# Moving four phi units out of the retention loop into the routing chain, and the first expert's w1 loads and splits ahead of the branch

## The chip, the cores and the metric

The kernel runs on one core of a Trainium2 chip. The metric is the device time of one launch in microseconds (us). TensorE (PE) multiplies matrices, PEld loads its weights, VectorE (DVE), ScalarE (ACT) and GpSimd (POOL) work element by element, SyncE (SP) issues most DMA transfers. Each engine works through its own instructions in order.

## The reference

Three stages are chained; everything is float32.

- Retention over 4 batches, 8 heads, 768 positions: `state = gamma * state + k v^T`, `y = q state / 8`. Its output is `x` with 3072 tokens of 512 features.
- A mixture of 8 experts with one expert per token: `e = argmax(x w_gate)`, then `relu(x w1[e]) w2[e]` times the gate probability and a sigmoid of `x w_output_gate`.
- A soft mixture: `logits = x phi` (32 slots), a softmax over tokens gathers slot inputs, 8 experts of 4 slots each transform them, a softmax over slots combines them.

## The kernel before

**Retention loop.** 24 iterations, one per tile of 128 tokens. SP loads 1 MB per tile (`load`), PE computes scores (L408), the output (L432, L441) and the state (L455). After every third tile the gates follow: `gate_mm` (L491), an ACT copy, `gate_sum` (L506), a chain of small DVE operations up to `sb` (L557), and `scale_mm` (L573), which needs `sb`. The tiles are written to DRAM as `xs` (`x_put`, L623).

**Phi units.** The soft mixture's logits need `w2[e] phi`, which doesn't depend on tokens. It is cut into 32 units of 512 KB of w2, four per expert (`wq_mm`, L232); after the fourth unit `wq_turn` transposes the sum on DVE and `wq_put` (L240) stores it. Units 0 to 15 run in the loop (`wq_load` in iteration i, `wq_mm` in iteration i+2), 16 to 23 are loaded in pairs of 1 MB in the loop's last four iterations and multiplied at its end, 24 to 31 run in the expert loop (`wq_early`, `wq_late`).

**Routing chain.** After the loop DVE counts and ranks the tokens, sorts the experts by size (`ordi`), and makes the row numbers `xidx`; POOL gathers the first expert's tokens from `xs` (`gather(0)`, L716). DVE then makes `limi`, the number of tokens over an expert's capacity.

**The branch.** Every engine loads `limi` into a register (L735), compares it with 0 and jumps over the overflow code (L825; the jump is taken with these inputs).

**Expert loop.** For each expert and each of 8 slices of 128 hidden units (a step g): `load_w` brings 256 KB of w1 (L209, three buffers `r1`), `split_w` makes a high part on ACT (L218) and a low part on DVE (L219), `l1` multiplies the three products on PE (L880, 12 matmuls) and ACT applies the relu (L885). Before the first step `x_mm` transposes the gathered tokens on PE (L858) and `x_split` splits them.

The order on each engine is written out by hand, as the calls stand. Each DMA of SP and ACT is given one of eight lanes in turn (DMAHW0 to 7), and is issued only when the earlier DMA of the same lane has landed.

Of the kernel before, what the change touches and what calls it, by code (L numbers as in the profile page):

```python
# [9 lines left out]
F32 = mybir.dt.float32  # L10
F32R = mybir.dt.float32r
BF16 = mybir.dt.bfloat16
I32 = mybir.dt.int32
ACTF = mybir.ActivationFunctionType
ALU = mybir.AluOpType
AX = mybir.AxisListType
# [5 lines left out]
DM = H * D  # L22
E = 8
FF = 1024
NS = 32
NCH = S // 128
NTILE = NT // 128
KD = DM // 128
# [7 lines left out]
NPRE, NX = 48, 4  # L36
NH = 8
NQ = 4 * E
NQL, NQ0 = 16, 24
GROUPS = [(t, 3) for t in range(0, 21, 3)] + [(21, 2), (23, 1)]  # L40
ENDS = {t + n - 1: (t, n) for t, n in GROUPS}
ORDER = "xe sc s m g1 gc xr w rr rs g2 G0 Gb q oq os st G1 rc rk xw k".split()
# [94 lines left out]
def retention_moe_kernel(ctx, tc, qt, kt, kn, vn, gates, moe_w1, moe_w2,  # L137
# [33 lines left out]
    pos = per.tile([128, NTILE], I32, name="pos")  # L171
    rt = per.tile([128, 3, E], F32, name="rt")
    ordi = per.tile([1, E], I32, name="ordi")
    cnt, ordf, over = (rt[:, i, :] for i in range(3))
    mrun = per.tile([128, 1], F32, name="mrun")
    srun = per.tile([128, 1], F32, name="srun")
# [15 lines left out]
    def load_er(k):  # L192
        if k < E:
            er.append(nc.values_load(ordi[0:1, k:k + 1], engines=[mybir.EngineType.SP], min_val=0, max_val=E - 1))
# [30 lines left out]
    def wq_mm(u, pool, tag):  # L225
        if not 0 <= u < NQ:
            return
        e, kk = divmod(u, 4)
        if kk == 0:
            wacc[e] = pool.tile([128, 256], F32, tag=tag, name="wps")  # L230
        for g, t in enumerate(wtt.pop(u)):
            nc.tensor.matmul(out=wacc[e][32 * g:32 * g + 32, :], lhsT=phi[:, kk, :], rhs=t,  # L232
                             start=(kk == 0), stop=(kk == KD - 1), skip_group_check=True)
# [33 lines left out]


    with ExitStack() as pa:
        io = pa.enter_context(tc.tile_pool(name="io", bufs=5))  # L270
        sc2 = pa.enter_context(tc.tile_pool(name="sc2", bufs=2))
        one = pa.enter_context(tc.tile_pool(name="one", bufs=1))
        pT = pa.enter_context(tc.tile_pool(name="pT", bufs=1, space=PSUM))

# [44 lines left out]
                                         scale=dc[:, c - 2, q:q + 1])  # L319

        wst = pa.enter_context(tc.tile_pool(name="wst", bufs=4))

        def wq_load(i):

            if i % 5 < 4 and i // 5 * 4 + i % 5 < NQL:
                e, q = divmod(i // 5 * 4 + i % 5, 4)
                t = wst.tile([128, FF], F32, tag="wt", name="wt")
                nc.sync.dma_start(out=t, in_=moe_w2[1, e, :, q * FF:(q + 1) * FF])
                wtt[4 * e + q] = [t[:, g * 256:g * 256 + 256] for g in range(4)]
            elif NTILE - 4 <= i < NTILE:  # L330
                e, q = divmod(NQL + 2 * (i + 4 - NTILE), 4)
                t = io.tile([128, 4 * DM], F32, tag="raw", name="wt2")
                nc.sync.dma_start(out=t, in_=moe_w2[1, e, :, q * FF:(q + 2) * FF])
                for h in range(2):
                    wtt[4 * e + q + h] = [t[:, h * FF + g * 256:h * FF + g * 256 + 256] for g in range(4)]

        def wq_at(i):
            if 2 <= i < 22 and (i - 2) % 5 < 4:
                return [(i - 2) // 5 * 4 + (i - 2) % 5]
            if NTILE - 2 <= i:  # L340
                return [NQL + 2 * (i + 2 - NTILE), NQL + 2 * (i + 2 - NTILE) + 1]
            return []
# [3 lines left out]
                wq_mm(u, pT, "w")  # L346
                wq_turn(u)

        def wq_early(u):

            if NQ0 <= u < NQ:
                e, q = divmod(u, 4)
                wtt[u] = []
                for h in range(2):
                    t = m2a.tile([128, 512], F32, tag="m2", name="wte")
                    nc.sync.dma_start(out=t, in_=moe_w2[1, e, :, q * FF + h * 512:q * FF + h * 512 + 512])
                    wtt[u] += [t[:, 0:256], t[:, 256:512]]

        def wq_turn(u):
            if u % 4 == 3 and 0 <= u < NQ0:  # L360
                pool, tag = (wraw, "r1") if u == NQ0 - 1 else (sc2, "ws")
                wput[u // 4] = pool.tile([128, KF, NS], F32, tag=tag, name="ws")
                nc.vector.transpose(out=wput[u // 4], in_=wacc.pop(u // 4).rearrange("p (f t) -> p f t", t=32))

        raw, k2, q2, sps, sS, Ops, xT3, xr3, gps, gts, gs, scl, gr, oz = ({} for _ in range(14))
# [168 lines left out]
        def gate_own(i):  # L534
            if i not in ENDS:
                return
            t, n = ENDS[i]
            sm = gs[t]
            og = gps[t][:, LG:LG + 16 * n].rearrange("p (u e) -> p u e", e=16)[:, :, E:2 * E]
            one_ = lambda k: sm[:, k, 0, 0:n]  # L540
            big = lambda k: sm[:, k, 0:n, :]
            nc.vector.tensor_tensor(out=big(4), in0=og, in1=oh[:, t:t + n, :], op=ALU.mult)
            nc.vector.tensor_reduce(out=one_(5), in_=big(4), axis=AX.X, op=ALU.add)
            nc.scalar.activation(out=one_(7), in_=one_(5), func=ACTF.Exp, scale=-1.0)
# [38 lines left out]
        def rank(i):  # L583
            if i not in ENDS:
                return
            t, n = ENDS[i]
            eng = nc.vector if t + n == NTILE else nc.gpsimd
            g = gps.pop(t)
            sm = sc2.tile([128, 3, 4, E], F32, tag="sm2", name="sm2")
            nc.vector.tensor_tensor(out=sm[:, 0:n, 0, :], in0=g[:, RK:RK + E * n].rearrange("p (u e) -> p u e", e=E),  # L590
                                    in1=oh[:, t:t + n, :], op=ALU.mult)
            ps = pos[:, t:t + n]
            with nc.allow_low_precision(reason="a single whole number under 2 ** 24 among zeros"):
                nc.vector.tensor_reduce(out=ps, in_=sm[:, 0:n, 0, :], axis=AX.X, op=ALU.add)
            lo = sc2.tile([128, 3], I32, tag="lo", name="lo")[:, 0:n]
            hi = sm[:, 0, 2, 0:n]
            nc.vector.tensor_scalar(out=lo, in0=ps, scalar1=127, scalar2=None, op0=ALU.bitwise_and)
            nc.vector.tensor_tensor(out=hi, in0=ps, in1=lo, op=ALU.subtract)
            nc.vector.tensor_tensor(out=lcol[:, t:t + n, 1, :], in0=each(con("code"), n), in1=bc(hi, n, 32), op=ALU.is_equal)
            eng.tensor_tensor(out=lcol[:, t:t + n, 0, :], in0=lcol[:, t:t + n, 1, :], in1=bc(con("till")[:, t:t + n], n, 32), op=ALU.mult)  # L600
            eng.tensor_scalar(out=lcol[:, t:t + n, 1, :], in0=lcol[:, t:t + n, 1, :], scalar1=con("row"), scalar2=None, op0=ALU.mult)
            nc.vector.tensor_tensor(out=lrow[:, t:t + n, :], in0=each(con("i128"), n), in1=bc(lo, n, 128), op=ALU.is_equal)
# [14 lines left out]
        def x_put(i, queues=(nc.sync,)):  # L617
            if i not in ENDS:
                return
            t, n = ENDS[i]  # L620
            x = xr3.pop(t)
            for a in range(4):
                queues[a % len(queues)].dma_start(  # L623
                    out=xs[t * 128:(t + n) * 128, a * 128:(a + 1) * 128].rearrange("(b q) d -> q b d", q=32),
                    in_=x[32 * a:32 * a + 32, 0:n].rearrange("q u b d -> q (u b) d"))
# [35 lines left out]
        i = NTILE - 1  # L661
        wq_put(0)
        x_put(i - 1, (nc.sync, nc.scalar))
        gate_own(i)
        for u in wq_at(NTILE):
            wq_mm(u, pT, "st")
# [1 line left out]
        nc.tensor.matmul(out=cp[:, 0:E], lhsT=ones, rhs=run[:, NTILE, :], start=True, stop=True)  # L668
        rank_mm(i)
        gate_scale(i)  # L670
        wq_mm(NQ0 - 2, pT, "st")
        scale_mm(i)
        c8 = one.tile([128, 3, E], F32, name="c8")
        sq8 = one.tile([128, 3, E, E], F32, name="sq8")
# [11 lines left out]
        nc.vector.tensor_tensor(out=sq8[:, 1], in0=sq8[:, 0], in1=con("iota").unsqueeze(1).to_broadcast(full), op=ALU.mult)  # L686
        nc.vector.tensor_reduce(out=ordf, in_=sq8[:, 1], axis=AX.X, op=ALU.add)
        nc.vector.tensor_copy(out=ordi, in_=ordf[0:1, :])
        rank(i)
        wq_mm(NQ0 - 1, pT, "st")  # L690
        lp = pT.tile([128, 64], F32, tag="s", name="lp", bufs=2)
        for u in range(NTILE):
            nc.tensor.matmul(out=lp, lhsT=lrow[:, u, :], rhs=lcol[:, u].rearrange("p a b -> p (a b)"),
# [25 lines left out]
                    bounds_check=NT, oob_is_err=False)  # L719

        gather(0)
        wq_turn(NQ0 - 1)


    with ExitStack() as pv:
        vs = pv.enter_context(tc.tile_pool(name="vs", bufs=1))
        vw = pv.enter_context(tc.tile_pool(name="vw", bufs=2))
        vp = pv.enter_context(tc.tile_pool(name="vp", bufs=2, space=PSUM))
        vy = pv.enter_context(tc.tile_pool(name="vy", bufs=1, space=PSUM))
        lim = vs.tile([1, E + 1], F32, name="lim")  # L730
        limi = vs.tile([1, E + 1], I32, name="limi")
        nc.vector.tensor_scalar(out=lim[:, 0:E], in0=over[0:1, :], scalar1=0.0, scalar2=None, op0=ALU.max)
        nc.vector.tensor_reduce(out=lim[:, E:E + 1], in_=lim[:, 0:E], axis=AX.X, op=ALU.max)
        nc.vector.tensor_copy(out=limi, in_=lim)
        most = nc.values_load(limi[0:1, E:E + 1], min_val=0, max_val=NT)  # L735

        def spill(k):
# [100 lines left out]

    whl = ctx.enter_context(tc.tile_pool(name="whl", bufs=3))
    xtp = ctx.enter_context(tc.tile_pool(name="xtp", bufs=NX))
    m2p = ctx.enter_context(tc.tile_pool(name="m2p", bufs=NPRE))
    hp = ctx.enter_context(tc.tile_pool(name="hp", bufs=NH))
# [2 lines left out]
    with ExitStack() as pb:  # L847
# [207 lines left out]
            ws = wput[e] = sp.tile([128, KF, NS], F32, tag="wp", name="ws", bufs=2)  # L1055
            nc.vector.transpose(out=ws, in_=wacc.pop(e).rearrange("p (f t) -> p f t", t=32))

        load_er(0)
        for g in range(3):
            load_w(g)  # L1060
        wq_put(0)
        for u in range(NQ0, NQ0 + 4):
            wq_early(u)
        for kk, ps in enumerate([x_mm(0, kk, "ABCD"[kk]) for kk in range(KD)]):
            if kk == 0:
                split_w(0)
            x_split(0, ps)
        split_w(1)
        load_er(1)
        for g in range(G):  # L1070
            e, f = divmod(g, KF)
# [235 lines left out]
```

## Time and profile before

| | us |
|---|---|
| median of 3 runs | 454.89 (454.47 to 457.6) |
| the profiled execution | 450.32 |
| its span, first to last instruction | 448.6 |
| PE busy in the span | 390.5 (87%) |
| DVE busy | 259.4 (58%) |
| ACT busy | 150.2 (33%) |

The profiled execution took 1.7 us more than its span and 4.57 us less than the median. Times of rows are us from the span's start. A row `A B engine line op out<-in xN [idle <-releaser]` starts at A and takes B; the bracket is the idle time before it and what ended it. A q behind an engine's name is its sequencer, which waits, branches and issues.

### The profile page before, as it was taken

The numbers are of one execution on the slowest core, as the hardware profiler recorded it, in microseconds if no ns is written. First come the engines' busy times: TensorE is split into PE (matmuls) and PEld (weight loads), VectorE is DVE, ScalarE is ACT, GpSimd is POOL, SyncE is SP. The second block draws the span as 40 slices with busy tenths as digits, with TensorE's granted clock in tenths as the row PEclk, the third lists the DMA queues.
The fourth block names the chain that finished last, engine by engine and source line by source line (L and its number), as shares of the span: only waits on it lengthen the run. The fifth ranks groups of instructions, "written<-read, shape, count | busy, mean of one in ns | idle before, by whom it ended". The sixth has DMA issues, their size and how long they took to land.

```text
span 448.6 us, 11522 instructions
## 1 busy us (share of the span) xinstructions
PE 390.5 (87%) x4395; PEld 289.2 (64%) x4395; DVE 259.4 (58%) x704; ACT 150.2 (33%) x347; POOL 128.4 (29%) x137
## 2 busy tenths in 40 slices
PE   2799998989754979999999999999999995893981
PEld 2676777767522757877877869877787862232551
DVE  1578888988871125566656567656677743322232
ACT  1432222222322134534434444444445421111232
POOL 1206544445413302306226061150704030200020
PEclk9999999999855889999999999999999998898896
DMA  8999999999945987795886958779793839999998
GB/s 269 386 416 408 366 311 400 369 378 356 289 110 141 319 316 237 249 334 163 268 306 220 316 185 295 275 253 319 231 321 131 290 127 344 384 368 366 382 345 281
DMA packets 72209, 132.58 MB, mean 296 GB/s; under 512 B 8306, under 2 KB 28784, under 8 KB 69328
## 3 DMA queue, kind: packets, MB, share of 16 engines
q1 hardware_dynamic: 64816, 119.98, 76.2%
q0 software_dynamic: 3344, 8.13, 5.8%
q10 hardware_dynamic: 3984, 3.63, 2.5%
q8 instruction: 37, 0.61, 0.5%
q14 instruction: 28, 0.23, 0.2%
HBM read 117.68 MB, written 14.05 MB: 294 GB/s over the span
## 4 chain that ended last, share of the span: by engine, by line
PE 68%; DMA 17%; SPq 4%; DVE 4%; ACT 3%; issue 2%; ACTq 1%; POOL 0%; POOLq 0%; DVEq 0%
PE hps L880 31%; PE gps L988 4%; DMA wt<-in_moe_w_dram 4%; PE xps L858 4%; PE fh L1163 4%; PE slo L1010 3%; PE lps L910 3%; PE so L1202 3%; PE o L441 3%; PE s L408 2%; DMA raw<-in_vn_dram 2%; SPq L623 2%; DMA raw<-in_kn_dram 2%; PE wps L232 2%; PE o L432 1%
## 5 line engine op out<-in xcount | busy, mean ns | idle before, releaser
L880 PE MATMUL hps<-xh,wh 128*128 128x416 f32 (+2 forms) x256 | 95.0, 371 | 2.6 <-ACT h L885 2.6
L880 PE MATMUL hps<-xl,wh 128*128 128x416 f32 (+2 forms) x256 | 90.0, 352 | 0.0
L880 PE MATMUL hps<-xh,wl 128*128 128x416 f32 (+2 forms) x256 | 89.9, 351 | 0.0
L219 DVE TENSOR_TENSOR wl<-r,wh 128x512 fp32r<-128x512 f32 x64 | 43.7, 683 | 62.9 <-ACT wh L218 61.7
L971 POOL DMA_INDIRECT ctok<-cn,xidx x29 | 28.7, 991 | 141.6 <-DVE cn L968 135.2
L885 ACT ACTIVATE h<-hps 128x416 f32<-128x416 f32 (+2 forms) x64 | 32.6, 510 | 89.8 <-PE hps L880 89.6
L880 PEld LDWEIGHTS hps<-xh,wh 128*128 128x128 f32 x256 | 48.9, 191 | 17.0 <-issue 11.6
L218 ACT ACTIVATE wh<-r 128x512 fp32r<-128x512 f32 x64 | 40.2, 628 | 32.6 <-DMA r<-in_moe_w_dram 17.8
L880 PEld LDWEIGHTS hps<-xl,wh 128*128 128x128 f32 x256 | 49.0, 192 | 1.9 <-issue 0.8
L880 PEld LDWEIGHTS hps<-xh,wl 128*128 128x128 f32 x256 | 49.0, 191 | 0.8
L716 POOL DMA_INDIRECT xg<-xs,xidx x29 | 29.9, 1032 | 50.6 <-PE xps L858 33.5
L418 DVE TENSOR_TENSOR sS<-s,csa 128x512 f32<-128x512 f32 x48 | 30.8, 684 | 22.7 <-PE s L408 22.7
L408 PE MATMUL s<-raw 64*128 64x128 f32 x384 | 30.1, 298 | 9.8 <-DMA raw<-in_qt_dram 9.6
L892 DVE STREAM_TRANSPOSE hB<-h 128x416 f32<-128x416 f32 (+2 forms) x64 | 34.4, 576 | 0.0
L408 PEld LDWEIGHTS s<-raw 64*128 64x128 f32 x384 | 25.1, 199 | 12.2 <-DMA raw<-in_qt_dram 5.7
L858 PE MATMUL xps<-cs,xg 128*128 128x128 f32 x116 | 19.9, 297 | 10.0 <-PEq L825 9.2
L473 ACT COPY xT<-o 128x512 f32<-128x512 f32 x24 | 13.9, 579 | 40.7 <-PE o L441 40.7
L441 PE MATMUL o<-sS,raw 128*64 128x128 f32 x384 | 27.1, 285 | 0.0
L390 POOL TENSOR_TENSOR k<-raw,cs 128x512 f32<-128x512 f32 x20 | 20.4, 1039 | 18.7 <-DMA raw<-in_qt_dram 18.7
L858 PEld LDWEIGHTS xps<-cs,xg 128*128 128x128 f32 x116 | 13.7, 148 | 17.6 <-issue 16.0
L988 PE MATMUL gps<-hB,pd 32*32 32x256 f32 x816 | 20.5, 414 | 3.8 <-DVE pd L942 3.8
L441 PEld LDWEIGHTS o<-sS,raw 128*64 128x64 f32 x384 | 21.2, 140 | 3.7 <-issue 3.4
(160 smaller groups left out, 551.7 us busy)
## 6 DMA issues: line engine op xcount, KB each, us to landing
m<-in_moe_w_dram SPq DMA_DIRECT2D x128, 256.0 KB, 5.4
r<-in_moe_w_dram SPq DMA_DIRECT2D x64, 256.0 KB, 4.0
w<-in_moe_w_dram SPq DMA_DIRECT2D x64, 256.0 KB, 4.7
wt<-in_moe_w_dram SPq DMA_DIRECT2D x16, 512.0 KB, 8.3
xs<-xr SPq DMA_DIRECT2D x28, 192.0 KB, 8.8
raw<-in_kt_dram SPq DMA_DIRECT2D x5, 1024.0 KB, 8.9
raw<-in_kn_dram SPq DMA_DIRECT2D x5, 1024.0 KB, 8.5
raw<-in_vn_dram SPq DMA_DIRECT2D x5, 1024.0 KB, 8.3
```

Source lines behind the costliest of these rows:

```text
L218: nc.scalar.activation(out=hi, in_=t, func=ACTF.Copy)
L219: nc.vector.tensor_tensor(out=lo, in0=t, in1=hi, op=ALU.subtract)
L408: nc.tensor.matmul(out=ps[h][:, p, :], lhsT=kq(i, p, 0)[r], rhs=kq(i, p, 1)[r], start=True, stop=True, tile_position=(64 * h, 0), skip_gro ...
L418: nc.vector.tensor_tensor(out=sS[i][:, h], in0=sps.pop((i, h)), in1=con("dm", 128)[:, 4 * h:4 * h + 4, :], op=ALU.mult)
L441: nc.tensor.matmul(out=o_at(i, p, h), lhsT=vals(i, 2 * p + h), rhs=s[:, h, p, :], start=(i % NCH == 0 and n < 4), stop=True, skip_group_ch ...
L716: nc.gpsimd.indirect_dma_start(out=xg[e][j][0:r, :], out_offset=None, in_=xs[:, :], in_offset=bass.IndirectOffsetOnAxis(ap=xidx[0:r, e, j: ...
L858: nc.tensor.transpose(out=ps[:, j * 128:j * 128 + r], in_=xg[e][j][0:r, kk * 128:(kk + 1) * 128], identity=ident[0:r, 0:r])
L880: nc.tensor.matmul(out=ps, lhsT=a[:, kk * 128:(kk + 1) * 128], rhs=x[e][kk][:, 0:c], start=(n == 0), stop=(n == 11))
L885: nc.scalar.activation(out=hs[g][:, 0:c], in_=ps, func=ACTF.Relu)
L892: nc.vector.transpose(out=hB[e][:, 0:NB[e], f, :], in_=hs[e * KF + f][:, 0:c].rearrange("p (b t) -> p b t", t=32))
L971: put = nc.gpsimd.indirect_dma_start(out=ctok[:, :], out_offset=bass.IndirectOffsetOnAxis(ap=xidx[0:r, e, j:j + 1], axis=0), in_=cn[0:r, j ...
L988: nc.tensor.matmul(out=ps[a][32 * j:32 * j + 32, :], lhsT=pd[q, b, :], rhs=hB[e][q, b].rearrange("p f t -> p (f t)"), start=(i == 0), stop ...
```

## The change

Units 0 to 11 now run in the loop (loads in iterations 0, 2, 3, 5, 7, 8, 10, 12, 13, 15, 17 and 18; before, sixteen of the first 19 iterations had one), 12 to 19 take the place of the last eight, and 20 to 23 are loaded in two pairs behind the loop: one between the two last stores of `xs`, one behind the first three w1 loads. Their matmuls stand behind `gather(0)`, ahead of the branch. The first expert number is read by SP and three slices of w1 are loaded ahead of the branch, and two of them are split there. `limi` is made ahead of the transposes. The sum of units 20 to 23 goes to `pd`, no longer to a buffer of `r1`. The pools `sc2` and `io` change places.

```diff
-NQL, NQ0 = 16, 24
+NQL, NQE, NQ0 = 12, 20, 24
...
+        steps = {i: n for n, i in enumerate(i for i in range(20) if i % 5 in (0, 2, 3))}
...
-                pool, tag = (wraw, "r1") if u == NQ0 - 1 else (sc2, "ws")
-                wput[u // 4] = pool.tile([128, KF, NS], F32, tag=tag, name="ws")
+                wput[u // 4] = pd[:, 0:KF, :] if u == NQ0 - 1 else sc2.tile([128, KF, NS], F32, tag="ws", name="ws")
...
         x_put(i - 1, (nc.sync, nc.scalar))
+        wq_pair(NQE)
         gate_own(i)
...
         nc.vector.tensor_copy(out=ordi, in_=ordf[0:1, :])
+        load_er(0)
+        for g in range(3):
+            load_w(g)
+        wq_pair(NQE + 2)
         rank(i)
...
         gather(0)
+        nc.vector.tensor_scalar(out=lim[:, 0:E], in0=over[0:1, :], scalar1=0.0, scalar2=None, op0=ALU.max)
+        nc.vector.tensor_reduce(out=lim[:, E:E + 1], in_=lim[:, 0:E], axis=AX.X, op=ALU.max)
+        nc.vector.tensor_copy(out=limi, in_=lim)
+        wq_turn(NQE - 1)
+        wq_put(0)
+        for u in range(NQE, NQ0):
+            wq_mm(u, pT, "w")
         wq_turn(NQ0 - 1)
+    whl = ctx.enter_context(tc.tile_pool(name="whl", bufs=3))
+    split_w(0)
+    split_w(1)
...
-        load_er(0)
-        for g in range(3):
-            load_w(g)
         wq_put(0)
         for u in range(NQ0, NQ0 + 4):
             wq_early(u)
```

SP at the end of the routing chain before (`xs<-xr` 32x8x128 and 32x4x128 are the two last stores):

```order
L240 DMA wps<-ws 128x256 [waits DMAHW6_49,DVE_49]
L623 DMA xs<-xr 32x8x128 [waits DMAHW7_49,Activation_49]
L623 DMA xs<-xr 32x8x128 [waits DMAHW0_49]
L623 DMA xs<-xr 32x4x128 [waits DMAHW1_49,DVE_49,Activation_49]
L623 DMA xs<-xr 32x4x128 [waits DMAHW2_49]
```

and now (the second 32x4x128 piece is on lane 6, which ACT's first 32x4x128 piece was given just before):

```order
L242 DMA wps<-ws 128x256 [waits DMAHW1_49,DVE_49]
L620 DMA xs<-xr 32x8x128 [waits DMAHW2_49,Activation_49]
L620 DMA xs<-xr 32x8x128 [waits DMAHW3_49]
L330 DMA wt_1801<-in_moe_w_dram 128x2048 [waits DMAHW4_49,PE_49]
L620 DMA xs<-xr 32x4x128 [waits DMAHW5_49,DVE_49,Activation_49]
L620 DMA xs<-xr 32x4x128 [waits DMAHW6_49]
L196 TENSOR_LOAD ordi [waits DVE_49]
...
L211 DMA r_1860<-in_moe_w_dram 128x512 [waits DMAHW7_49]
...
L330 DMA wt_1866<-in_moe_w_dram 128x2048 [waits DMAHW2_49,PE_49]
L242 DMA wps<-ws 128x256 [waits DMAHW3_49,DVE_49]
L742 TENSOR_LOAD limi [waits DVE_49]
```

A 1 MB pair now stands ahead of the last store, and the register load of `ordi`, three w1 loads (one of them shown), the second pair and a store of phi sums stand ahead of the branch.

PE at the branch before (`lp` are the ranking's last matmuls):

```order
L693 LDWEIGHTS lrow [waits DVE_49]
L693 MATMUL lp<-lcol,lrow 128x64
L735 TENSOR_LOAD limi [waits DMAHW3_49,DMAHW2_49,DMAHW4_49,DMAHW1_49,DMAHW5_49,DMAHW0_49,DMAHW6_49,DVE_49,DMAHW7_49,PE_49,Pool_49]
L825 COMPARE_AND_BRANCH
L743 TENSOR_LOAD limi
```

and now:

```order
L695 LDWEIGHTS lrow [waits DVE_49]
L695 MATMUL lp<-lcol,lrow 128x64
L234 MATMUL wps<-wt,phi 32x256 [waits DMAHW4_49,PE_49]
L234 MATMUL wps<-wt,phi 32x256 x7
L234 MATMUL wps<-wt,phi 32x256 [waits DMAHW2_49]
L234 MATMUL wps<-wt,phi 32x256 x7
L742 TENSOR_LOAD limi [waits DVE_49]
L832 COMPARE_AND_BRANCH
```

Two waits for a pair's DMA and sixteen matmuls stand ahead of PE's register load.

ACT at the branch now (before, the register load followed the two stores):

```order
L620 DMA xs<-xr 32x4x128 [waits Activation_49]
L620 DMA xs<-xr 32x4x128
L220 ACTIVATE wh_1969<-r_1860 128x512 [waits DMAHW3_49,DMAHW2_49,DMAHW4_49,DMAHW1_49,DMAHW5_49,DMAHW0_49,DMAHW6_49,DVE_49,DMAHW7_49,PE_49,Pool_49]
L220 ACTIVATE wh_1973<-r_1862 128x512 [waits DMAHW0_49]
L742 TENSOR_LOAD limi [waits DVE_49]
L832 COMPARE_AND_BRANCH
```

The first split waits for all eight lanes; lane 3 is that of SP's store of phi sums behind the second pair.

## Rows read from the trace of the kernel before

**Rows 1.** Busy time by stretch: PE, PEld, DVE, ACT, POOL, clock, DMA share, GB/s.
```profile
24.00:114.00 90.00, 84.69 (x1484) 66.54 (x1482) 75.84 (x232) 23.29 (x62) 42.16 (x46) 1.00 1.02 374
```

**Rows 2.** Chain of waits: start, us, what.
```profile
48.56 0.57 PE wps L232 x8
...
129.14 2.33 DMA xs<-xr
...
136.72 4.21 DMA xg<-xs,xidx
...
153.02 6.32 DMA r<-in_moe_w_dram
...
167.26 1.86 PE wps L232 x32
169.12 5.06 PE hps L880 x24
```

**Rows 3.** Timeline of PE, iterations 3 and 6 of the loop (with and without a unit).
```profile
27.15 0.84 PE L506 MATMUL g<-csa,gsb 128*128 128x16 f32 x6 [0.17 <-ACT gsb L499]
...
40.14 0.84 PE L506 MATMUL g<-csa,gsb 128*128 128x16 f32 x6 [0.60 <-ACT gsb L499]
```

**Rows 4.** Timeline of PE, iteration 13.
```profile
71.41 0.39 PE L573 MATMUL g<-sb,cs 128*128 128x12 f32 x2 [1.17 <-DVE sb L557]
```

**Rows 5.** Timeline of all engines, iteration 19.
```profile
97.27 0.17 DVE L557 TENSOR_TENSOR sb<-csa,sm 128x12 f32<-128x12 f32 x1
...
97.48 0.64 PE L232 MATMUL wps<-wt,phi 128*32 128x256 f32 x8 [1.40 <-DMA wt<-in_moe_w_dram]
...
98.22 0.37 PE L573 MATMUL g<-sb,cs 128*128 128x12 f32 x2
```

**Rows 6.** Timeline of SP, routing chain to the third expert step.
```profile
127.31 2.29 SPq L623 DMA_DIRECT2D xs<-xr  x4
139.89 4.82 SPq L209 DMA_DIRECT2D r<-in_moe_w_dram  x3
...
145.44 7.21 SPq L1049 DMA_DIRECT2D wte<-in_moe_w_dram  x10
```

**Rows 7.** Timeline of ACT, its pieces of the last store.
```profile
128.71 0.85 ACTq L623 DMA_DIRECT2D xs<-xr  x2
```

**Rows 8.** Line L735: duration in ns (min/median/max), first and last start.
```profile
L735 PEldq TENSOR_LOAD <-limi x1: 488/488/488, 134.3 to 134.3; - x1
```

**Rows 9.** Line L825, the jump, columns as in rows 8.
```profile
L825 ACTq EVENT_SEMAPHORE  x2: 17/17/17, 137.7 to 137.8; - x2
...
L825 ACTq COMPARE_BRANCH  x1: 50/50/50, 134.8 to 134.8; - x1
...
L825 PEldq COMPARE_BRANCH  x1: 4207/4207/4207, 134.9 to 134.9; - x1
```

**Rows 10.** Timeline of PE, routing chain to the first expert step.
```profile
122.70 1.94 PE L232 MATMUL wps<-wt,phi 128*32 128x256 f32 x16
...
139.77 0.88 PE L858 MATMUL xps<-cs,xg 128*128 128x128 f32 x3 [9.21 <-PEq L825]
...
142.59 2.62 PE L858 MATMUL xps<-cs,xg 64*128 64x64 f32 x9 [0.42 <-issue]
145.14 0.74 PE L880 MATMUL hps<-xh,wh 128*128 128x448 f32 x1
```

**Rows 11.** Timeline of PE, third and fourth expert step.
```profile
154.15 3.81 PE L232 MATMUL wps<-wte,phi 128*32 128x256 f32 x32
...
160.53 0.47 PE L880 MATMUL hps<-xh,wh 128*128 128x448 f32 x1 [2.56 <-ACT h L885]
```

**Rows 12.** L880 by stretch: PE and PEld busy, clock, DMA share, GB/s.
```profile
145.10:148.30 3.20, 3.16 (x9) 2.83 (x10) 0.51 0.80 188
...
160.50:165.40 4.90, 4.87 (x16) 4.39 (x17) 0.65 0.87 306
```

**Rows 13.** Line L209 from 139 to 142 us, the w1 loads.
```profile
DMA to landing us min/median/max: 3.4/3.4/3.4
```

**Rows 14.** DMA issues from 20 to 118 us: count, KB each, median us to landing.
```profile
wt<-in_moe_w_dram SPq DMA_DIRECT2D x4, 1024.0 KB, 8.5
```

More of the change, by code (lines that the diff above doesn't have):

```diff
@@ L173, in retention_moe_kernel @@
     ordi = per.tile([1, E], I32, name="ordi")
+    lim = per.tile([1, E + 1], F32, name="lim")
+    limi = per.tile([1, E + 1], I32, name="limi")
     cnt, ordf, over = (rt[:, i, :] for i in range(3))
@@ L269, in retention_moe_kernel @@
     with ExitStack() as pa:
+        sc2 = pa.enter_context(tc.tile_pool(name="sc2", bufs=2))
         io = pa.enter_context(tc.tile_pool(name="io", bufs=5))
-        sc2 = pa.enter_context(tc.tile_pool(name="sc2", bufs=2))
         one = pa.enter_context(tc.tile_pool(name="one", bufs=1))
@@ L321, in retention_moe_kernel, with wq_pair @@
         wst = pa.enter_context(tc.tile_pool(name="wst", bufs=4))
+        steps = {i: n for n, i in enumerate(i for i in range(20) if i % 5 in (0, 2, 3))}
+        def wq_pair(u):
+            e, q = divmod(u, 4)
+            t = io.tile([128, 4 * DM], F32, tag="raw", name="wt2")
+            nc.sync.dma_start(out=t, in_=moe_w2[1, e, :, q * FF:(q + 2) * FF])
+            for h in range(2):
+                wtt[u + h] = [t[:, h * FF + g * 256:h * FF + g * 256 + 256] for g in range(4)]
         def wq_load(i):
-            if i % 5 < 4 and i // 5 * 4 + i % 5 < NQL:
-                e, q = divmod(i // 5 * 4 + i % 5, 4)
+            if i in steps:
+                e, q = divmod(steps[i], 4)
                 t = wst.tile([128, FF], F32, tag="wt", name="wt")
@@ L330, in wq_load @@
             elif NTILE - 4 <= i < NTILE:
[L331 to L335, printed above, removed]
+                wq_pair(NQL + 2 * (i + 4 - NTILE))
         def wq_at(i):
-            if 2 <= i < 22 and (i - 2) % 5 < 4:
-                return [(i - 2) // 5 * 4 + (i - 2) % 5]
+            if i - 2 in steps:
+                return [steps[i - 2]]
             if NTILE - 2 <= i:
@@ L347, in wq_step @@
                 wq_turn(u)
[L349 to L357, printed above, removed]
         def wq_turn(u):
             if u % 4 == 3 and 0 <= u < NQ0:
-                pool, tag = (wraw, "r1") if u == NQ0 - 1 else (sc2, "ws")
-                wput[u // 4] = pool.tile([128, KF, NS], F32, tag=tag, name="ws")
+                wput[u // 4] = pd[:, 0:KF, :] if u == NQ0 - 1 else sc2.tile([128, KF, NS], F32, tag="ws", name="ws")
                 nc.vector.transpose(out=wput[u // 4], in_=wacc.pop(u // 4).rearrange("p (f t) -> p f t", t=32))
@@ L670, in retention_moe_kernel @@
         gate_scale(i)
-        wq_mm(NQ0 - 2, pT, "st")
+        wq_mm(NQE - 2, pT, "st")
         scale_mm(i)
@@ L688, in retention_moe_kernel @@
         nc.vector.tensor_copy(out=ordi, in_=ordf[0:1, :])
+        load_er(0)
+        for g in range(3):
+            load_w(g)
+        wq_pair(NQE + 2)
         rank(i)
-        wq_mm(NQ0 - 1, pT, "st")
+        wq_mm(NQE - 1, pT, "st")
         lp = pT.tile([128, 64], F32, tag="s", name="lp", bufs=2)
@@ L729, in retention_moe_kernel @@
         vy = pv.enter_context(tc.tile_pool(name="vy", bufs=1, space=PSUM))
[L730 to L734, printed above, removed]
         most = nc.values_load(limi[0:1, E:E + 1], min_val=0, max_val=NT)
@@ L836, in retention_moe_kernel @@
                 spill(k)
-    whl = ctx.enter_context(tc.tile_pool(name="whl", bufs=3))
     xtp = ctx.enter_context(tc.tile_pool(name="xtp", bufs=NX))
@@ L1063, in retention_moe_kernel @@
             wq_early(u)
-        for kk, ps in enumerate([x_mm(0, kk, "ABCD"[kk]) for kk in range(KD)]):
-            if kk == 0:
-                split_w(0)
+        for ps in [x_mm(0, kk, "ABCD"[kk]) for kk in range(KD)]:
             x_split(0, ps)
-        split_w(1)
         load_er(1)
```

## The prediction

> **What bounds the kernel now.** I read the granted clock and the busy shares by stretch first, then the chain of waits, then the timelines of the two places that the change touches. In the loop PE is busy 84.7 of 90 us at full clock while the DMA engines are busy all the time at 374 GB/s [rows 1]: two resources are nearly level, and PE's own work sets the pace. A unit of phi takes PE 0.57 us there [rows 2].
>
> Behind the loop the bound is a row of latencies. PE runs out of work and stands still for 9.21 us, until its sequencer is through the jump [rows 10]. Transposes follow until 145.14, then three expert steps to 154.15; then PE waits piecemeal for `wte` (3.81 us for work that takes 1.86 later [rows 2, 11]), stands still for 2.56 us more [rows 11] because the fourth slice of w1 was issued at 153.02 and took 6.32 us [rows 2], and its clock is at half speed for part of two stretches [rows 12]. SP issued that slice late since it stood behind the w1 loads (4.82 us for three: the third needs a buffer that the first split frees) and ten `wte` loads (7.21 us) [rows 6]. From 167.26, the second `wq_late`, PE works on without a stall; what the change is worth is read at this point.
>
> **The loop.** Iterations 3, 8, 13 and 18 lose a unit.
> - Iteration 8 has no gate work: 0.57 us of PE are saved.
> - Iterations 3 and 18 have gates; there the unit fills the wait for ACT's copy. With a unit 0.17 us of that wait are left, without one 0.60 [rows 3], so 0.43 of 0.57 come back: 0.14 saved in each.
> - In iteration 13 PE waits 1.17 us for `sb` right behind the unit [rows 4]. DVE is late there whatever PE does: 0.
> - In iteration 19 the unit that stays waits 1.40 us for its load [rows 5]. With 2 MB less to move (4 x 512 KB, 5.6 us at 374 GB/s) I take that wait as gone. PE would then be ready for L573 near 96.8, but `sb` ends at 97.44 and L573 now starts at 98.22 [rows 5]. DVE is late next: 98.22 - 97.50 = 0.7 saved.
>
> Sum 0.57 + 0.28 + 0 + 0.7 = 1.6 us. Bounds: 0, if DVE takes up all of it, and 4 x 0.57 + 1.40 = 3.7. I take 1.6, since both waits for DVE are in the rows.
>
> **The routing chain**, in times of the trace before. SP's second piece of the last store waits for the lane of ACT's first piece, issued at 128.71 [rows 7], which takes about 2.33 us like the row of this store [rows 2]; so it goes out near 131.0, not at 129.14. The stores are all landed some 1.9 us later, and the gathers move by as much: the fourth lands at 136.72 + 4.21 + 1.9 = 142.8. SP then reads `ordi` (0.49 [rows 8] and register work, together about 0.9), and issues three w1 loads from 132.4 at 0.72 apiece (7.21/10 [rows 6]), the second pair at 134.5 and the store of phi sums behind it.
>
> When does this pair land? A lone 256 KB load took 3.4 us in this quiet stretch [rows 13], of which 0.7 is bytes at 374 GB/s, so 2.7 are fixed. From 132.4, 2.7 + 1.84 MB/374 GB/s = 4.9 give 140.0; the gathers share the engines, so 140.5. Bounds: 134.5 + 3.4 = 137.9, as fast as the lone load, and 134.5 + 8.5 = 143.0, as in the full loop [rows 14]. I take 140.5: with 16 DMA engines mostly free it is nearer to the quiet row.
>
> By the Trainium skill, DMA: Bandwidth & Descriptors, section Anatomy of one DMA, a transfer takes 2.0 us plus its bytes at 436 GB/s. For 1 MB that is an estimate of 4.4 us, a landing at 138.9, and a sum 1.6 us lower; the lone load's 3.4 us is above its 2.6, so I stay with the rows.
>
> **The branch.** Before, no engine had work between `limi` and the jump. Now PE holds its register load until the pair has landed and two units are issued. At half clock two units take 1.94 us [rows 10]; the sequencer is free when the last one starts, so about 1.4. Then 0.49 for the register [rows 8], 4.2 for the jump (PE's compare-and-branch lasts 4207 ns; ACT, whose register load ends with PE's near 134.8, has its next instruction at 137.7, 2.9 us later [rows 8, 9]), and 0.7 to the first transpose (139.1 to 139.77): 6.8 in all. PE leaves at 147.3 instead of 139.77, **7.5 us later**. The cover that hides the moved units' work (1.94 us for the last two, as much for the first two near 133) is PE's 9.21 us of idleness; their wait is not covered.
>
> By the Trainium skill, Advanced Engine Details and Errata, section Control Flow Timing, a compare-and-branch takes about 108 ns. By that the jump would cost nothing and the sum would be 4.1 us lower; PE's row of 4207 ns speaks against it.
>
> ACT waits for the store of phi sums (about 141.5), splits twice (near 143), and is out of the jump 3.5 us later. DVE follows PE's last unit with a transpose and two low parts, to about 144, and is out near 148.5. Both are in time: `x_split` needs PE's transposes, which end later. The gathers (142.8) are in time too. So the two splits moved ahead save nothing at this point: PE was the last to be ready there before (145.14), and is so now.
>
> **What comes back.** Sixteen transposes at half clock: 2.62/9 each [rows 10], 4.7 us, so the first step starts at 152.0, not 145.14. SP, which leaves the branch near 139, now issues a store that waits for DVE's transpose (about 142.5) and then ten `wte` loads until 150, and the fourth slice near 151. It has a free buffer at once, and lands well before PE needs it at 161. Both stalls are gone. Then five steps at 5.06/2 = 2.53 [rows 2] and one `wq_late` at 1.86 [rows 2] give 14.5 us. Before, the clock cost 3.2 x 0.49 = 1.6 and 4.9 x 0.35 = 1.7 us [rows 12]; the second fall came behind the idle time at 158, which is gone. For the first I take 0.8, half, as the transposes now run without the gaps that they had. So 152.0 + 14.5 + 0.8 = 167.3 against 167.26: **the gain of some 7.5 us behind the branch is what PE's later exit costs. It breaks even** when PE leaves 7.5 us later, and I find just that.
>
> Bounds of this part: pair at 137.9 (-2.6), PE's jump as short as ACT's (-1.3), no clock loss (-0.8): -4.7. Pair at 143.0 (+2.5), clock loss as before (+0.8): +3.3.
>
> Everything else is moved in time alone. From 167 on PE's order is the same, and the work of the tail waits for buffers that the expert loop frees.
>
> **Sum.** -1.6 + 0.0. The profiled execution takes 450.32, so 448.7. It lies 4.57 below the median of the timed runs, 454.89; the difference is taken over: 453.3 us.
>
> **Rivals.**
> 1. *PE gets out of the branch early.* The pair lands about as fast as a lone load, or PE's jump is as short as ACT's. For it: the DMA engines have little else to do, and one engine's jump took 2.9 us. Against it: 0.8 MB of w1 stand ahead in SP's queue, and the 4207 ns row. The price is the lower bound, 454.89 - 1.6 - 4.7 = 448.6. Chance 0.23. A jump that costs nothing, as the page of the Trainium skill on Control Flow Timing (Advanced Engine Details and Errata) has it, would also belong here, with 453.3 - 4.1 = 449.2; as the 4207 ns row speaks against it, it has 0.02 of that chance.
> 2. *The wait for the last pair takes the place of the stall.* The place is PE's second wait for a pair, in front of its register load; from a landing at 140.5 + 1.6 = 142.1 on, every microsecond is a microsecond lost on the whole. If it lands at 143.0 with a queue as slow as in the loop, the clock stays low as before, and DVE swallows the loop's gain, that is 454.89 + 3.3 = 458.2; a second held lane (about 2 us) would make it 460. For it: xs pieces, pairs, w1 and gathers share eight lanes, and one lane is held already. Against it: the quiet row. Over 1% slower: chance 0.09; a loss below that: 0.15.
> 3. *The change moves work but not time.* The 2 MB were hidden, iteration 8's gain is lost in DVE's wait of iteration 13, and the seam is even: 454.9. Chance 0.15, inside 1%.
>
> My forecast itself has 0.38. About 1% (4.5 us) is what a measurement of this kernel can tell from no change. Forecast, rival 3 and the small loss lie inside; rival 1 is faster by over 1% in most of its part, and a larger gain of the loop with a middling seam adds some of it: 0.25 faster, 0.65 within, 0.10 slower. The range, leaving out a tenth at either end, goes from rival 1 to rival 2: 448.3 to 458.0.
>
> **What would show it.** In the changed trace: PE idle before its first transpose ended by its sequencer, the transposes starting over 5 us later against the loop's end than now; L573 of iteration 19 straight behind `sb`; the loop's last output (L441) 1 to 2 us earlier; no idle time behind the first `wq_late`, and no second fall of the clock. I am wrong if PE's transposes start less than 5 us later or if PE still waits for the fourth slice; and about the loop if its end moves by over 3 us.

## The result, and the profile after

| | before | changed |
|---|---|---|
| median, 20 runs each on one chip | 454.82 us (452.39 to 458.72) | 462.46 us (457.35 to 465.98) |
| ratio | | 1.013, interval 1.0099 to 1.016 |
| the profiled execution | 450.32 us | 461.11 us |
| its span | 448.6 us | 459.3 us |

The change makes the kernel 1.3% slower, about 5.9 us; 453.3 was forecast, with a range to 458.0. The ratio counts only executions within 1.5% of the fastest of their kernel, all 20 before and 13 of the changed kernel's; the medians of all 20 are 1.7% apart. Single executions scatter by several microseconds, also behind the second `wq_late`, where all kernels do the same work: that rest takes 279.7 to 284.9 us in the thirteen profiled executions of this document, 281.4 before and 284.9 now. So the two spans (10.7 us apart) overstate the loss, and I read it in one stretch, from the end of the ranking's last matmul (`lp`) to the start of the second `wq_late`:

```profile
167.19 1.93 PE L232 MATMUL wps<-wte,phi 128*32 128x256 f32 x32
```

```profile
174.36 1.93 PE L234 MATMUL wps<-wte,phi 128*32 128x256 f32 x32
```

Before it is 130.56 to 167.19, 36.6 us; now 131.31 to 174.36, 43.1 us. These 6.4 us are the loss in this pair of executions.

SP at the end of the routing chain in the changed kernel (start, duration, instruction, count; it answers to [rows 6]):

```profile
129.00 0.43 SPq L330 DMA_DIRECT2D wt<-in_moe_w_dram  x1
129.53 5.85 SPq L620 DMA_DIRECT2D xs<-xr  x2
136.46 1.47 SPq L211 DMA_DIRECT2D r<-in_moe_w_dram  x3
138.03 0.37 SPq L330 DMA_DIRECT2D wt<-in_moe_w_dram  x1
138.49 0.38 SPq L242 DMA_DIRECT2D wps<-ws  x1
```

The two pieces of the last `xs` store span 5.85 us: the second is out at 135.08, not at 131.0 as forecast. It waits for the lane of ACT's first piece, issued at 129.46, half a microsecond behind the 1 MB pair of 129.00. That piece took 5.6 us to land instead of the 2.33 of [rows 2]. The second pair follows at 138.03.

PE in the same stretch (in brackets the idle time before, and what ended it; it answers to [rows 10]):

```profile
131.08 0.23 PE L695 MATMUL lp<-lcol,lrow 128*128 128x64 bf16 x1 [0.89 <-DVE lrow L599]
134.90 1.93 PE L234 MATMUL wps<-wt,phi 128*32 128x256 f32 x16 [3.58 <-DMA wt<-in_moe_w_dram]
147.07 1.94 PE L234 MATMUL wps<-wt,phi 128*32 128x256 f32 x16 [10.24 <-SPq L832]
154.05 4.55 PE L864 MATMUL xps<-cs,xg 128*128 128x128 f32 x16 [5.05 <-DVEq L832]
```

The second pair is there at 147.04, 9.0 us after its issue (the releaser named is a row of SP's sequencer that waits for the same lane; what ended both is the pair's landing). The transposes start at 154.05, 22.7 us behind the ranking where they started 9.2 behind it before. Their last wait is for DVE to come out of the branch. DVE, ACT and the branch (L832; its rows give duration as min/median/max and the start):

```profile
149.07 0.45 DVE L360 STREAM_TRANSPOSE pd<-wps 128x256 f32<-128x256 f32 x1 [14.06 <-PE wps L234]
149.53 1.29 DVE L221 TENSOR_TENSOR wl<-r,wh 128x512 fp32r<-128x512 f32 x2
```

```profile
148.87 1.15 ACT L220 ACTIVATE wh<-r 128x512 fp32r<-128x512 f32 x2 [19.44 <-SPq L832]
```

```profile
L832 PEldq COMPARE_BRANCH  x1: 3787/3787/3787, 147.7 to 147.7; - x1
L832 DVEq COMPARE_BRANCH  x1: 72/72/72, 150.9 to 150.9; - x1
L832 DVEq EVENT_SEMAPHORE  x2: 21/21/21, 153.8 to 153.9; - x2
```

PE's own jump is over at 151.5. DVE takes it at 150.9. Ahead of it stand the transpose of the last sum, which waits for PE's units until 149.07, and two low parts, which wait for ACT's high parts; ACT waits until 148.5 for the store of phi sums issued at 138.49. DVE is through at 153.8, and that releases PE.

The chain of waits behind it (it answers to [rows 2, 11]):

```profile
154.05 4.55 PE xps L864 x16
158.60 8.91 PE hps L886 x36
167.51 1.86 PE wps L234 x32
169.37 5.06 PE hps L886 x24
```

No stall is left: `wq_late` takes 1.86 at once, and the steps follow without idle time.

### The profile page after: what moved, and what is told of

Read it like the earlier page. It is cut to its first block, busy times and chain, and to the rows that moved or that the text cites. A ratio compares the mean times of both kernels' runs of the same rounds, so it can differ in the third digit from the quotient of the medians.

```text
span 459.3 us, 11496 instructions
## 1 busy us (share of the span) xinstructions
PE 391.5 (85%) x4395; PEld 288.3 (63%) x4395; DVE 261.4 (57%) x704; ACT 150.3 (33%) x347; POOL 128.0 (28%) x137
## 4 chain that ended last, share of the span: by engine, by line
PE 57%; DMA 3%; DVE 3%; ACT 1%; issue 1%; another core or an unknown queue 0%; ACTq 0%; DVEq 0%; SPq 0%
PE hps L886 30%; PE gps L994 4%; PE xps L864 4%; PE slo L1016 3%; PE fh L1163 3%; PE lps L916 3%; PE so L1202 3%; PE lsum L932 2%; DMA ct<-ctok 1%; PE gsum L1007 1%; DMA m<-in_moe_w_dram 1%; PE ops L1256 1%; PE wps L234 1%; DMA out_dram<-ot 1%; DVE hB L898 1%
## 5 line engine op out<-in xcount | busy, mean ns | idle before, releaser
L415 DVE TENSOR_TENSOR sS<-s,csa 128x512 f32<-128x512 f32 x48 | 30.8, 685 | 21.3 <-PE s L405 21.2
L405 PE MATMUL s<-raw 64*128 64x128 f32 x384 | 30.8, 303 | 10.7 <-DMA raw<-in_qt_dram 10.7
L405 PEld LDWEIGHTS s<-raw 64*128 64x128 f32 x384 | 25.7, 202 | 13.1 <-DMA raw<-in_qt_dram 5.7
L234 PE MATMUL wps<-wt,phi 128*32 128x256 f32 x192 | 17.1, 454 | 13.8 <-SPq L832 10.2
L1018 DVE SCALAR_TENSOR_TENSOR acc<-acc,smb,slo 128x512 f32<-128x512 f32 x8 | 6.0, 747 | 34.2 <-PE lsum L932 17.0
```

Source lines behind the costliest of these rows:

```text
L405: nc.tensor.matmul(out=ps[h][:, p, :], lhsT=kq(i, p, 0)[r], rhs=kq(i, p, 1)[r], start=True, stop=True, tile_position=(64 * h, 0), skip_gro ...
L415: nc.vector.tensor_tensor(out=sS[i][:, h], in0=sps.pop((i, h)), in1=con("dm", 128)[:, 4 * h:4 * h + 4, :], op=ALU.mult)
```

## The experiments

My theory: the whole loss lies ahead of PE's register load, in the late landing of the last pair. Rivals: the w1 part costs it; DVE's and ACT's work ahead of the branch costs it. Every ratio is against runs of the kernel before on the same chip; the intervals are 95%.

| kernel | PE starts after the ranking, us | ranking to second `wq_late`, us | ratio (interval) |
|---|---|---|---|
| before | 9.2 | 36.6 | 1 |
| changed | 22.7 | 43.1 | 1.013 (1.010 to 1.016) |
| w1 part alone | 9.4 | 30.6 | 0.988 (0.983 to 0.993) |
| w1 part alone, again | 9.2 | 31.3 | 0.986 (0.983 to 0.990) |
| phi part alone | 16.6 | 38.4 | 1.004 (1.000 to 1.008) |
| store first | 19.8 | 41.0 | 1.008 (1.004 to 1.012) |
| no second pair | 16.8 | 37.8 | 1.003 (0.999 to 1.006) |
| no pairs | 13.5 | 34.8 | 0.994 (0.991 to 0.997) |
| no pairs, splits behind | 9.6 | 31.7 | 0.992 (0.989 to 0.996) |
| loop light | 9.4 | 37.5 | 1.002 (0.998 to 1.005) |
| w1 alone, splits behind | 9.1 | 30.8 | 0.982 (0.976 to 0.988) |
| w1 alone, `limi` early | 9.1 | 32.3 | 0.981 (0.975 to 0.987) |
| w1 alone, both | 8.3 | 31.7 | 0.984 (0.980 to 0.987) |

**The w1 part alone** (on the kernel before):

```diff
         nc.vector.tensor_copy(out=ordi, in_=ordf[0:1, :])
+        load_er(0)
+        for g in range(3):
+            load_w(g)
...
+    split_w(0)
+    split_w(1)
```

(`limi` and the sum in `pd` as in the changed kernel.)

> The kernel before with the w1 part alone: expert number, three w1 loads and two splits ahead of the branch, limi ahead of the transposes; all phi units stay where they were. Theory (the loss lies in the last pair of phi weights ahead of PE's register load): PE leaves the branch within 1 us of the 139.8 us of before, wte and the fourth slice of w1 are issued about 5 us earlier, the two stalls (1.95 and 2.56 us) and the second fall of the clock (1.7 us) go: about 449 us, 5 to 6 us faster than before. Rival (the splits ahead of the branch hold ACT and DVE, and PE's first transpose waits for DVE's jump): PE starts 3 us or more later, 454 us or slower.

445.61 us against 450.39, 0.988. PE:

```profile
142.62 2.70 PE L863 MATMUL xps<-cs,xg 128*128 128x128 f32 x9 [9.44 <-PEq L831]
156.37 1.93 PE L234 MATMUL wps<-wte,phi 128*32 128x256 f32 x32
158.72 0.47 PE L885 MATMUL hps<-xh,wh 128*128 128x448 f32 x1 [0.42 <-ACT h L890]
163.78 1.93 PE L234 MATMUL wps<-wte,phi 128*32 128x256 f32 x32
```

PE starts as soon behind the ranking as before, and what were 3.81 and 2.56 us in [rows 11] is 1.93 and 0.42. The rival falls: this part gains, 5.4 us by the ratio. Run again on another chip:

> The w1 part alone, two splits ahead of the branch, beside the next run on the same chip: 1.2% below before, as measured; up to 1.8% if the difference from the run with the splits behind (1.8%) was the chip's.

447.08 against 453.64, 0.986 (0.983 to 0.990).

**The phi part alone** (the changed kernel, w1 loads and splits behind the branch):

```diff
-        load_er(0)
-        for g in range(3):
-            load_w(g)
         wq_pair(NQE + 2)
...
-    split_w(0)
-    split_w(1)
```

> The changed kernel without the w1 part: w1 loads and splits are behind the branch again, the two pairs of phi weights stay in the routing chain. Theory: the last pair has 0.75 MB less ahead of it and lands near 144 instead of 147; PE starts its transposes near 149, 9 us later than before, 6 of which come back as stalls behind the branch go: about 456 us, 1 to 2 us slower than before. Rival (the w1 part brings the loss): at or below 454 us.

452.44 against 450.39, 1.004, as the theory has it: about 2 us slower.

```profile
131.96 5.86 SPq L620 DMA_DIRECT2D xs<-xr  x2
137.92 0.36 SPq L330 DMA_DIRECT2D wt<-in_moe_w_dram  x1
```

```profile
143.40 1.94 PE L234 MATMUL wps<-wt,phi 128*32 128x256 f32 x16 [4.02 <-DMA wt<-in_moe_w_dram]
150.14 1.78 PE L859 MATMUL xps<-cs,xg 128*128 128x128 f32 x6 [4.80 <-DMA xg<-xs,xidx]
```

The store's lane is held just as long. The pair lands 5.5 us after its issue, with three slices of w1 less ahead of it, instead of 9.0. PE's own jump and DVE's:

```profile
L826 PEldq EVENT_SEMAPHORE  x2: 51/51/51, 148.1 to 148.3; - x2
L826 DVEq EVENT_SEMAPHORE  x2: 21/21/21, 149.9 to 150.0; - x2
```

DVE is last here too, 6.6 us behind the landing, with no split ahead of the branch: it jumps behind the transpose of the last sum. The gathers, which the row of PE names, had all landed by 149.8.

The two parts don't add up. From the ranking to the second `wq_late`, w1 alone takes 6.0 us less than before, phi alone 1.8 more, both together 6.4 more. Both take away the same stalls: from PE's start to the second `wq_late` it is 27.4 us before, 21.2 with w1 alone, 21.8 with phi alone and 20.3 with both. PE's start, which is 0.2 and 7.4 us later with one of them, is 13.5 later with both.

**The store first:**

```diff
-        wq_pair(NQE)
...
         x_put(i, (nc.sync, nc.scalar))
+        wq_pair(NQE)
```

> The changed kernel with the first of the two pairs (units 20, 21) issued behind the last store of xs instead of ahead of it. If the held lane of the store (out at 135.1 instead of the 131.0 forecast) is what makes the last pair late: the pair lands 4 us earlier, about 457 us. If the bytes are (two pairs, three slices of w1 and four gathers, 3.7 MB at 0.33 MB per us are 11 us, whatever their order): the pair still lands near 145.5, about 459.5 us, 1 to 1.5 us faster than the changed kernel.

454.42 against 450.39, 1.008: by the ratios 2.3 us better than the changed kernel, between the two cases. SP and PE:

```profile
129.40 2.26 SPq L620 DMA_DIRECT2D xs<-xr  x4
133.03 0.35 SPq L330 DMA_DIRECT2D wt<-in_moe_w_dram  x1
136.01 0.37 SPq L330 DMA_DIRECT2D wt<-in_moe_w_dram  x1
```

```profile
145.74 1.94 PE L234 MATMUL wps<-wt,phi 128*32 128x256 f32 x16 [5.62 <-SPq L832]
152.55 4.55 PE L864 MATMUL xps<-cs,xg 128*128 128x128 f32 x16 [4.88 <-DVEq L832]
```

All four pieces go out in 2.26 us: no lane is held once the pair stands behind. But the second pair still takes 9.7 us, and PE has it 13.0 us behind the ranking instead of 15.7; 9.9 was forecast. So this order takes away 2.7 of the 5.8 us. It also puts the first pair's megabyte among the later loads, so what the lane costs by itself is not measured.

**No second pair:**

```diff
         wq_pair(NQE)
+        same = [wtt[NQE], wtt[NQE + 1]]
...
-        wq_pair(NQE + 2)
+        wtt[NQE + 2], wtt[NQE + 3] = same
```

> The changed kernel without the load of the last pair: units 22 and 23 multiply the weights of 20 and 21 (so the sum of the sixth expert is left wrong). Theory: PE's register load comes at about 138.8 instead of 147.1, PE's transposes start near 147.5 (DVE's jump is then last), 6 us earlier than in the changed kernel: 454 to 455 us. Rival (the DVE and ACT work ahead of the branch, or the 1 MB pair ahead of the stores, set PE's start): under 2 us faster than the changed kernel, 459 us or more.

452.06 against 450.39, 1.003. PE starts 5.9 us earlier than in the changed kernel, the theory said 6; the time is some 4.6 us less.

```profile
137.06 3.64 PE L234 MATMUL wps<-wt,phi 128*32 128x256 f32 x32 [3.30 <-DMA wt<-in_moe_w_dram]
150.54 4.55 PE L865 MATMUL xps<-cs,xg 128*128 128x128 f32 x16 [9.84 <-DVEq L833]
```

```profile
145.58 1.15 ACT L220 ACTIVATE wh<-r 128x512 fp32r<-128x512 f32 x2 [13.71 <-DMA wps<-ws]
```

PE is done at 140.7 and then waits for DVE. ACT begins to split at 145.58, when the store of phi sums has landed. PE still starts 7.6 us later than before, with DVE's jump last, as expected. So beside the late pair there is a second cause: what ACT and DVE wait for ahead of the branch.

**No pairs:**

```diff
+        same = [wtt[NQE - 2], wtt[NQE - 1]]
+        wtt[NQE], wtt[NQE + 1] = wtt[NQE + 2], wtt[NQE + 3] = same
...
-        wq_pair(NQE)
...
-        wq_pair(NQE + 2)
```

> The changed kernel without the loads of both pairs in the chain: units 20 to 23 multiply the weights of 18 and 19 (the sum of the sixth expert is left wrong). The stores of xs, the w1 part and the lighter loop stay. Theory (the two pairs are the whole loss): the last store goes out without a held lane, PE starts its transposes about as soon after the loop as in the run of the w1 part alone, and the time is 1.2% below before, plus what the lighter loop gives (0 to 0.3%). Rival (something else in the changed chain, as the splits or the sum in pd, costs 2 us or more): 0.7% below before or less.

451.7 against 454.57, 0.994. The rival was right: PE still starts 4 us later than with the w1 part alone, so the pairs are not the whole loss.

```profile
139.92 1.15 ACT L220 ACTIVATE wh<-r 128x512 fp32r<-128x512 f32 x2 [10.43 <-DMA wps<-ws]
```

```profile
144.89 4.55 PE L864 MATMUL xps<-cs,xg 128*128 128x128 f32 x16 [10.35 <-DVEq L832]
```

**No pairs, splits behind the branch** tests this cause by itself (the same kernel, `split_w(0)` and `split_w(1)` between the `x_split`, as before):

> The changed kernel without both pairs' loads (units 20 to 23 multiply the weights of 18 and 19), and with the two splits behind the branch. In the run without the pairs PE was through its own jump at 140.4 and began at 144.9, when DVE was through: ACT and DVE had waited until 139.6 ahead of their splits for the store of the phi sums. If this is a cost of its own (a third beside the two pairs): PE begins 9 to 9.6 us after the ranking's last matmul instead of 13.5, and the time is about 1.4% below before instead of 0.6%. If PE's start hangs on something else: no difference, 0.6% below before.

```profile
141.11 1.79 PE L861 MATMUL xps<-cs,xg 128*128 128x128 f32 x6 [6.04 <-PEq L828]
```

PE starts 9.6 us behind the ranking, as forecast, and its own jump is last again. In the traces the stretch to the second `wq_late` is 3.1 us shorter. The time, 449.89 against 453.64 (0.992), fell less than I said; on two chips the step from 0.994 is inside the intervals. It also stays 2.8 us above the w1 part alone on the same chip (447.08), of which the stretch shows 0.4; where the rest lies is open.

**Loop light** (the kernel before):

```diff
+        if u < NQL and kk == 3:
+            return
...
-            if i % 5 < 4 and i // 5 * 4 + i % 5 < NQL:
+            if i % 5 < 3 and i // 5 * 4 + i % 5 < NQL:
```

> The kernel before with four phi units left out altogether, load and matmuls, in iterations 3, 8, 13 and 18 (their sums lack a quarter); nothing is moved and nothing else is changed. It gives what the loop alone gains. My forecast of the loop: 1.6 us, 0.35% below before. Rival (the loop's pace is set by what is behind PE, the gain is lost at the next wait): 0 to 0.5 us, no difference. If DMA set the pace, 2 MB at 374 GB/s less would be 5.6 us, 1.2%.

455.38 against 454.57, 1.002 (0.998 to 1.005): no gain, the rival's case; up to 1 us could hide in the interval.

This run is not quite the changed loop. It leaves out the loads of iterations 3, 8, 13 and 18, whose matmuls stand two iterations later, in 5, 10, 15 and 20; the changed kernel lacks the matmuls of 3, 8, 13 and 18. What those are worth is read in its own loop, from one iteration's scores (L408, now L405) to the next's. Six executions have all units: before and the five with w1 alone. Six have the changed loop: changed and the five runs made from it.

| iteration | all units, us | changed loop, us | forecast to be saved, us |
|---|---|---|---|
| 3 | 5.40 | 5.40 | 0.14 |
| 8 | 3.75 | 3.18 | 0.57 |
| 10 | 4.21 | 4.72 | 0 |
| 13 | 5.55 | 5.55; in three 7.1 | 0 |
| 18 | 4.81 | 4.80 | 0.14 |
| 19 | 4.99; in two 5.57 and 5.68 | 5.02 | 0.7 |

The executions agree within 0.02 us but for the ones named. Iteration 8 gains the whole unit, and iteration 10 loses 0.51 of it again, where PE now waits for `sb`. These are the rows before and now:

```profile
55.07 0.18 DVE L528 SCALAR_TENSOR_TENSOR sm<-sm,csa 128x24 f32<-128x24 f32 x1
58.37 0.37 PE L573 MATMUL g<-sb,cs 128*128 128x12 f32 x2
```

```profile
55.09 2.04 POOL L387 TENSOR_TENSOR k<-raw,cs 128x512 f32<-128x512 f32 x2
56.14 1.03 DVE L525 SCALAR_TENSOR_TENSOR sm<-sm,csa 128x24 f32<-128x24 f32 x1
59.93 0.39 PE L570 MATMUL g<-sb,cs 128*128 128x12 f32 x2 [0.35 <-DVE sb L554]
```

One DVE operation on the way to `sb` takes 1.03 us instead of 0.18. It ends at 57.17, just after POOL's operations of that time (57.13); no run tests whether POOL holds it. Iteration 19 is longer, by the 1.40 us wait for `wt` of [rows 5], in two of the six executions with all units, those whose fourth tile began by 20.3 us; in the four where it began after 22.8 the wait is at most 0.5. This wait made up nearly half of the gain that I forecast for the loop.

Iteration 13 takes 7.1 us in phi alone, store first and no second pair, all three on one chip. PE, without its unit, idles there for 0.40 and 1.29 us, and its matmuls behind are slow:

```profile
73.83 0.39 PE L570 MATMUL g<-sb,cs 128*128 128x12 f32 x2 [1.29 <-DVE sb L554]
75.10 1.98 PE L438 MATMUL o<-sS,raw 128*64 128x128 f32 x16
```

(phi alone; in the changed kernel's own trace this o<-sS,raw takes 1.09). The granted clock is 0.57 from 74 to 78 us there, so part of this stretch ran at the lower level. The other three executions idle as long and keep the full clock; what decides is open. So the lighter loop gains nothing, and loses some 1.6 us where the clock falls.

The four units' 2.3 us of PE went into waits for the gates' ACT and DVE work. PE's waits from 24 to 116 us, before and now (total, times, longest):

```profile
PE g L506 <- ACT gsb L499: 2.0, 7, 0.6
PE g L573 <- DVE sb L557: 1.8, 2, 1.2
```

```profile
PE g L570 <- DVE sb L554: 2.9, 4, 1.3
PE g L503 <- ACT gsb L496: 2.9, 7, 0.6
PE g L563 <- DVE sm L539: 0.4, 1, 0.4
```

That is 3.8 us before, 3.8 to 4.4 in the six executions with all units, and 6.2 in each of the six of the changed loop.

**w1 alone, splits behind**, and **w1 alone with `limi` early** (the operations that make `cnt`, `over` and `limi` moved ahead of `xidx` of the other experts):

> The w1 part alone again, but with the two splits behind the branch and only the three w1 loads ahead of it. Theory (it is the early issue of wte and of the fourth slice that pays): within 0.3% of the run with the splits ahead, 1.0 to 1.3% below before. Rival (the splits ahead of the branch give the gain themselves): half of the gain or less, 0 to 0.6% below before.

447.33 against 454.57, 0.982: the gain needs no split ahead of the branch.

```profile
139.55 0.98 PE L860 MATMUL xps<-cs,xg 128*128 128x128 f32 x2 [9.09 <-DVEq L827]
161.30 1.93 PE L234 MATMUL wps<-wte,phi 128*32 128x256 f32 x32
```

> The w1 part alone, and limi made before the row numbers of the other experts (seven DVE operations of 0.15 to 0.5 us stand behind it instead of ahead). PE, SP and POOL load their register about 1.1 us earlier; the gathers are not later. If PE's start hangs on its jump: 0.7 to 1.1 us faster than the w1 part alone, 1.4% below before. If it hangs on the gathers' landing (the fourth at 143.1, half a microsecond after PE's start): no difference from it, 1.2% below before.

448.21 against 454.57, 0.981. PE's own jump is over at 139.2, but PE starts at 140.70, 9.1 us behind the ranking, when DVE is through (140.5), and then waits 1.90 us for a gather: the earlier register load is eaten by DVE's exit and the gathers. Both together:

> The best of what was run, put together: three w1 loads ahead of the branch, the splits behind it, limi ahead of the row numbers of the other experts, all phi units where they were before. 1.8% below before, as each of the two alone gave; if the earlier limi and the later splits add up, 2.0% or more; PE begins about 9 us after the ranking's last matmul in any case, since its jump takes 4 us.

446.66 against 453.64, 0.984 (0.980 to 0.987). PE starts 8.3 us behind the ranking, not 9, but the two don't add up in the time. These three cannot be told apart; each beats the kernel before by 1.6 to 1.9% and the changed one by some 3%. The simplest is three loads of w1 ahead of the branch, splits behind it, phi units left alone.

## Why the prediction was wrong, point by point

- **The bound** was read rightly: what the change is worth was decided between the ranking and the second `wq_late`, and the 6.4 us there agree with the 5.9 measured.
- **The loop, -1.6 us:** wrong, nothing was gained. I priced each iteration by itself. Iteration 8's 0.57 came, but 0.51 of it was lost in a wait for DVE, as rival 3 has it, though in iteration 10 and not 13. Iterations 3 and 18 are not shorter at all, where I took 0.14 each. I had PE's own work set the loop's pace; where gates stand, it does not. The 0.7 of iteration 19 was a wait for `wt` that four of six executions don't have. Iteration 13's 0 was right, but the fall of the clock there, 1.6 us in three of six executions, I did not see.
- **The held lane, store out at 131.0:** right mechanism, too early. It went out at 135.08; 0.7 of the 4.1 us are the later place of the whole chain in this trace. I priced ACT's piece at the 2.33 us of a row with no megabyte ahead of it, while the change puts one there: 5.6.
- **The last pair, 140.5, bounds 137.9 to 143.0: the step that failed.** It landed at 147.04. Of 6.5 us, 0.7 are the later place of the chain, 2.8 the later issue behind the held lane. The other 3.0 are bytes that I had left out: the sum had 1.84 MB and half a microsecond for the gathers. The DMA view of 136.4 to 147.1 shows them:

```profile
DMA packets 958, 2.80 MB, mean 262 GB/s; under 512 B 128, under 2 KB 242, under 8 KB 826
q0 software_dynamic: 253, 0.82, 22.3%
```

  2.80 MB moved at 262 GB/s, 0.82 MB of them the gathers'. My own rule with these bytes, 2.7 us and 2.80 MB at 374 GB/s, gives an estimate of 10.2 us from the first w1 issue to the landing; 10.6 were measured. No run left the gathers out, so their share is worked out, not measured. "Nearer to the quiet row" was the wrong choice: with three slices of w1, the pair, a store and four gathers in one place the stretch isn't quiet. That row is not a lone load either, since another w1 load was issued 0.6 us ahead of it. The pair's 9.0 us is near the loop's 8.5.
- **PE's exit 6.8 us after the landing:** 7.0 measured, but by another path, so the agreement is luck. PE's register load came 0.1 us behind the landing, not 1.4, and its own jump was over after 4.5 us; then it waited for DVE. I had DVE and ACT "in time" since `x_split` comes after the transposes, and missed that the first transpose itself waits until DVE has left the branch. By that, my own 148.5 for DVE would already have held PE's 147.3. No pairs, with the splits ahead and behind, shows the wait: 13.5 against 9.6 us.
- **What comes back:** right. From the first transpose to the second `wq_late` it took 27.4 us before and takes 20.3; 20.0 was forecast. Both stalls and the second fall of the clock are gone. Of the first fall more stays than the 0.8 I took: the granted clock is 0.50 from 158.5 to 161.4, which costs some 1.4 us.
- **The chances.** Rival 2 is what happened. In the stretch alone it breaks even at a landing at 140.5; 147.04 is 146.3 in the times of the trace before, so 5.8 us are lost, and with 0.2 at PE's exit and 0.3 behind it that is 6.3 of the 6.4 measured. I gave a loss of over 1% only 0.09: the upper bound had the loop's 8.5 us, but from an issue at 134.5.

## What to carry to other kernels

Before work is moved into an idle stretch, add up all the bytes that will be in flight there, gathers included, and what must land ahead of the wait that ends it: an idle engine is not an idle queue. In this kernel PE left the branch only when DVE had, so nothing that waits for a DMA should stand ahead of such a branch on any engine, not even a transpose of what another engine makes behind the DMA. And a change of two parts should be run part by part: here one gained 5.4 us alone, the other lost about 2, and together they lost 5.9.

## What was not expected of the hardware

The jump's cost isn't fixed. From the compare to the sequencer's next instruction ACT and DVE took 2.8 and 2.9 us in the changed kernel, behind the pairs' landing, SP 5.7 us in the midst of the transfers (139.53 to 145.22), and POOL, which jumped with SP, 5.6. PE's row was 3.8 us there, 4.2 before [rows 9], and 5.05 in the run without pairs, whose jump falls into the gathers. That the code is itself loaded by DMA would fit: the DMA view has a queue of kind instruction, and two of its packets stand at 143.6 in the midst of SP's and POOL's jump. No run here takes that apart.
